# Gelus of the first block held as copies and made in one row, with one conversion buffer and a lower fill goal

## The chip, the cores and the metric

One core of one Trainium2 chip. The metric is the device time of the whole kernel in microseconds (us), lower is better.

## The reference, cut to what matters

```python
# attention: q, k, v of (batch 8, heads 8, seq 576, head_dim 64)
scores = scale * q @ k.T
scores = np.where(scores >= max(scores) - tau, scores, -1e9)
attn = exp(scores - max(scores)); attn = attn / (attn.sum() + 1e-9)
x = (attn @ v), transposed to (4608 tokens, 512)
# MLP: d_model 512, d_ff 2048, exact gelu
return gelu(x @ w_in) @ w_out
```

## The kernel before

Attention runs in **slots**: a slot is one chunk of 128 queries (or the 64 left over) of one pair of heads. The first batch, slots 0 to 19, covers four pairs; its probabilities are turned (transposed, and divided by their sums on the way) by TensorE with a diagonal of the reciprocal sums, from slot 20 on by VectorE and transfers. VectorE also converts the weights, which come as 64-bit floats, within the first batch. Whatever TensorE time is left is filled with matmuls of the MLP: a block is 256 tokens, and `GOAL` says how many blocks should be done by which slot. A block's layer one (`hT`) needs gelus, and each gelu needs another table of ScalarE than the exps of the softmax. `table()` puts the exp's table back by a dummy exp. In the lines of the profile, `sc` are scores, `tr` turned probabilities in PSUM (the memory into which the matmuls of this kernel write), `pT` their copy outside it, `diag` the diagonal, `xT` the attention's result in PSUM and `x` its copy, `g` a gelu's result, `o_ps` layer two. An engine *stands* while it idles for another's result or buffer; the *row* is the eight gelus that the change makes one after another.

```python
    late = []
    lag = [1]
    dirty = [False]
    def gelus(left):
        while len(late) > left:
            g, j, hT = late.pop(0)
            t = gp.tile([P, 2, TOK], FP32, tag="g", name="g")
            nc.scalar.activation(t, hT, AF.Gelu)
            g[j - 1], g[j] = t[:, 0, :], t[:, 1, :]
            dirty[0] = True
    def table():
        if dirty[0]:
            nc.scalar.activation(warm[:, 1:2], warm[:, 0:1], AF.Exp)
            dirty[0] = False

    def block_steps(n):
        g = {}
        mlp["layer"] = 1
        for j in range(N_DF):
            if j % 2 == 0:
                hT = None
            for c in range(N_DM):
                yield NS_IN, (j * P // PIECE + 1) * N_DM
                if hT is None:
                    hT = ps.tile([P, 2, TOK], FP32, tag="mm", name="hT")
                nc.tensor.matmul(hT[:, j % 2, :], lhsT=w_in_sb[c][:, j * P:(j + 1) * P], rhs=x_blk[n][:, c, :],
                                 start=(c == 0), stop=(c == N_DM - 1))
            if j % 2:
                late.append((g, j, hT))
                gelus(lag[0])
        for m in range(TOK // P):
            for j in range(N_DF):
                mlp["layer"] = 2
                yield NS_OUT, len(pieces) - N_DF + j + 1
                if j not in g:
                    gelus(0)
                if j == 0:
                    o = ps.tile([P, 512], FP32, tag="mm", name="o_ps")
                nc.tensor.matmul(o[:, 0:d_model], lhsT=g[j][:, m * P:(m + 1) * P], rhs=w_out_sb[j],
                                 start=(j == 0), stop=(j == N_DF - 1))
            o_sb = op.tile([P, d_model], FP32, tag="o_sb", name="o_sb")
            nc.scalar.copy(o_sb, o[:, 0:d_model])
            row = n * TOK + m * P
            nc.sync.dma_start(out[row:row + P, :], o_sb)
    # ... (cut)
    GOAL = [(-1, 0.0), (START - 1, 0.0), (BATCH - 1, 0.55)]      # BATCH = 20, START = 10
```

In each slot (cut; the whole order matters, since every engine takes its instructions in this order):

```python
        early = p < EARLY
        last = slots[n - 1] if 0 < n <= len(slots) else None
        if p < NP:
            scores(p, i)
            softmax_head(p, i)
        elif n == len(slots):
            ext = weights_in()
        if not early or n % 2 == 0:
            gelus(0)
            table()
        # ... weigh_v of what is due; if early: fill(owed, tokens); table()
        # ... turn_p_early of the slot before; softmax_tail
        convert(3000 if n < 2 * HP else 3650 if n < BATCH - 1 else 1e9)
        if early:
            diagonal(p, i)
```

The turn of the first batch and the conversion of a piece of weights (cut):

```python
    def turn_p_early(p, i):
        s = st[p]
        if i == 0 or (p < HP and i == 2):
            s["pT"] = [one.tile([P, KR, S], FP32, tag=f"pT{e}", name=f"pT{e}") for e in range(2)]
        w, diag = s.pop(("p", i)), s.pop(("diag", i))
        n = 1 if i == NC else 2
        def turn(to, cols, e):
            nc.tensor.matmul(to, lhsT=w[:, cols], rhs=diag[:, e, :], start=True, stop=True)
        for e in range(n):
            tr = ps.tile([P, NC, P], FP32, tag="mm", name="tr")
            for c in range(NC):
                at = e * (S + TAIL) + c * P
                turn(tr[:, c, :], slice(at, at + P), e)
            if i < NC:
                nc.scalar.copy(s["pT"][e][:, 0:NC, i * P:(i + 1) * P], tr)
        if i == NC:
            for e in range(2):
                nc.vector.tensor_copy(s["pT"][e][:, 0:NC, MAIN:S], tr[:, :, e * TAIL:(e + 1) * TAIL])
        tails = s["pT"][0][:, NC, :]
        tr = ps.tile([P, NC, P], FP32, tag="mm", name="tr")
        if i < NC:
            for e in range(2):
                at = MAIN + e * TAIL
                turn(tr[e * TAIL:(e + 1) * TAIL, 0, :], slice(at, at + TAIL), e)
            nc.scalar.copy(tails[:, i * P:(i + 1) * P], tr[:, 0, :])
            return
        turn(tr[0:TAIL, 0, :], slice(MAIN, S), 0)
        for e in range(2):
            rows = slice(e * TAIL, (e + 1) * TAIL)
            nc.vector.tensor_copy(tails[rows, MAIN:S], tr[0:TAIL, 0, rows])
```

```python
        vec = nc.vector
        ahead = None
        while raws or ahead:
            piece = None
            if raws:
                dst, raw, shifted = raws.pop(0)
                hi = raw.rearrange("p (f w) -> p f w", w=2)[:, :, 1]
                top = shifted.rearrange("p (f w) -> p f w", w=2)[:, :, 0]
                expo, power = (gp.tile([P, PIECE], U32, tag="g", name=s) for s in ("expo", "power"))
                vec.tensor_scalar(expo, hi, 0x7FF00000, None, op0=ALU.bitwise_and)
                nc.scalar.activation(power, expo, AF.Relu, bias=rebias, scale=8.0)
                piece = dst, hi, top, power
                yield 340
            if ahead:
                dst, hi, top, power = ahead
                mant = gp.tile([P, PIECE], U32, tag="g", name="mant")
                vec.tensor_scalar(mant, top, 0x0FFFFFFF, 0x10000000, op0=ALU.bitwise_and, op1=ALU.bitwise_or)
                yield 340
                vec.scalar_tensor_tensor(power, hi, 0x80000000, power, op0=ALU.bitwise_and, op1=ALU.bitwise_or)
                yield 720
                vec.scalar_tensor_tensor(dst, mant, 2.0 ** -28, power.bitcast(FP32), op0=ALU.mult, op1=ALU.mult)
                load_piece()
                converted[0] += 1
                yield 700
            ahead = piece
```

`ps` has four buffers of tag "mm" in PSUM, shared by `hT`, `o_ps`, `xT` and the turns' `tr`; `gp` has ten buffers of tag "g", shared by the gelus' results and the scratch of the conversions.

## Time and profile before

| | before |
|---|---|
| median of 3 runs | 1420.45 us (1420.29 to 1422.51) |
| span of the profiled run | 1421.8 us |
| TensorE busy / idle | 1382.1 / 39.7 us |
| ScalarE table loads in the trace | 144 of 1.283 us |

The profile's page gives busy time by engine and by fortieths of the span; tables of stretches give the same for any stretch, with the granted clock of TensorE; the list of waits says which instruction ended an engine's idle time (engine, tile and line that waited, what it waited for, then us in total, times, longest); the timeline has each instruction with its start, length and, in brackets, the idle time before it and what ended that. The lines that matter stand in the prediction. One more of before, the timeline of TensorE at the worst wait (start, length, what, count):

```profile
149.31 1.05 PE L302 MATMUL tr<-diag,p 128*128 128x128 f32 x8
152.65 2.70 PE L302 MATMUL tr<-diag,p 128*128 128x128 f32 x12 [2.28 <-ACT g L509]
155.28 2.29 PE L356 MATMUL sc<-pd_tail,q_tail 128*128 128x288 f32 x4
157.36 4.50 PE L543 MATMUL o_ps<-w_out,g 128*128 128x512 f32 x8
```

TensorE stands 2.28 us in the middle of a turn, until the gelu on ScalarE gives a PSUM buffer back; after it, four score matmuls take 2.29 us where the same four take 1.24 at 129.09, since the clock has fallen.

### The profile page before, as it was taken

Reading aid. Unit: us, or ns where it says so; the run is one execution under the profiler, and the core shown is the slowest. Engines: PE = TensorE matmul, PEld = TensorE weight load, DVE = VectorE, ACT = ScalarE, POOL = GpSimd, SP = SyncE. Lnnn points to the kernel's source line nnn. Section 1 sums busy time; section 2 is a strip of 40 time slices with the busy share of each in tenths; the row PEclk is TensorE's granted clock in tenths of the full one; section 3 lists DMA queues with packets and bytes.
Section 4 is the critical chain, followed back from the end, with each engine's and each line's share of the span. In section 5 each row is a group of like instructions: output and inputs, shape, how many; then the busy total and the mean of one; then the engine's idle time right before and its main releaser. Section 6 shows DMA issues by size and latency. Waiting matters only on the chain.

```text
span 1421.8 us, 19662 instructions
## 1 busy us (share of the span) xinstructions
PE 1382.1 (97%) x6544; PEld 958.8 (67%) x6544; DVE 892.6 (63%) x1788; ACT 640.9 (45%) x1040; POOL 388.0 (27%) x812
## 2 busy tenths in 40 slices
PE   6898999999999999999999999999999999999999
PEld 4666547566466574665756647566588888888887
DVE  5887777777777777777777777777764142241330
ACT  5758525436356273462645727547141140230320
POOL 4443244434433433434434434430000000000000
PEclk9999999999999999999999999999999999999999
DMA  9977167776666676666766666674500000001000
GB/s 265 295 264 243 38 145 150 148 156 129 134 136 148 146 156 129 146 135 149 162 148 146 158 146 150 141 160 101 106 3 8 23 1 26 19 1 48 12 8 23
DMA packets 219347, 167.05 MB, mean 117 GB/s; under 512 B 122480, under 2 KB 203952, under 8 KB 219248
## 3 DMA queue, kind: packets, MB, share of 16 engines
q1 hardware_dynamic: 193040, 108.65, 36.2%
q0 software_dynamic: 23808, 56.57, 13.1%
q8 instruction: 53, 0.87, 0.3%
q10 hardware_dynamic: 2400, 0.59, 0.2%
q14 instruction: 46, 0.38, 0.1%
HBM read 71.68 MB, written 11.47 MB: 58 GB/s over the span
## 4 chain that ended last, share of the span: by engine, by line
PE 87%; DVE 5%; ACT 5%; DMA 2%; issue 1%; SPq 0%; POOL 0%; DVEq 0%; ACTq 0%; POOLq 0%
PE bank L663 27%; PE o_ps L543 18%; PE hT L530 18%; PE sc L356 12%; PE xT L473 10%; ACT p L371 1%; DVE p L387 1%; PE tr L302 1%; DVE power L187 1%; DMA q<-in_q_dram 1%; DVE nmx L368 1%; ACT L509 1%; ACT diag L401 1%; DMA turned_p<-in_moe_w_in_dram 1%; ACT power L179 0%
## 5 line engine op out<-in xcount | busy, mean ns | idle before, releaser
L371 ACT ACTIVATE p<-sc,nmx 128x576 f32<-128x576 f32 x288 | 202.4, 739 | 383.9 <-DVE nmx L368 383.8
L368 DVE TENSOR_REDUCE nmx<-sc 128x1 f32<-128x576 f32 x288 | 205.0, 749 | 158.8 <-PE sc L356 158.7
L530 PE MATMUL hT<-x,w_in 128*128 128x256 f32 x1280 | 296.2, 384 | 0.0
L543 PE MATMUL o_ps<-w_out,g 128*128 128x512 f32 x640 | 295.1, 604 | 0.0
L530 PEld LDWEIGHTS hT<-x,w_in 128*128 128x128 f32 x1280 | 238.4, 190 | 56.4 <-issue 24.7
L387 DVE SCALAR_TENSOR_TENSOR p<-sc,thr,p 128x576 f32<-128x576 f32 x288 | 225.4, 816 | 65.2 <-ACT p L371 64.1
L369 POOL TENSOR_SCALAR thr<-nmx,tau_eff 128x1 f32<-128x1 f32 x288 | 84.3, 293 | 547.7 <-DVE nmx L368 547.6
L543 PEld LDWEIGHTS o_ps<-w_out,g 128*128 128x128 f32 x640 | 117.1, 190 | 140.0 <-issue 138.2
L356 PE MATMUL sc<-kT,qT 64*128 64x288 f32 x960 | 165.9, 435 | 2.8 <-DVE p L387 2.5
L473 PE MATMUL xT<-pT,v 128*64 128x256 f32 (+1 forms) x1280 | 163.7, 409 | 2.7 <-ACT g L509 2.7
L434 DVE STREAM_TRANSPOSE turned_p<-p 128x1152 f32<-128x1152 f32 x112 | 154.1, 1376 | 3.0
L356 PEld LDWEIGHTS sc<-kT,qT 64*128 64x128 f32 x960 | 93.7, 188 | 84.2 <-issue 71.8
L473 PEld LDWEIGHTS xT<-pT,v 128*64 128x64 f32 x1280 | 89.8, 137 | 74.1 <-issue 12.7
L234 POOL DMA_DIRECT2D v<-in_v_dram x208 | 110.5, 534 | 10.7 <-issue 9.8
L663 PE MATMUL bank<-x,w_in 128*128 128x256 f32 x384 | 93.3, 379 | 0.0
L663 PE MATMUL bank<-w_out,unit 128*128 128x256 f32 x416 | 92.4, 379 | 0.0
L516 ACT ACT_TABLE_LOAD x71 | 91.1, 1283 | 1.3
L509 ACT ACT_TABLE_LOAD x71 | 91.1, 1283 | 1.2
L663 PEld LDWEIGHTS bank<-w_out,unit 128*128 128x128 f32 x416 | 79.0, 190 | 10.7
L663 PEld LDWEIGHTS bank<-x,w_in 128*128 128x128 f32 x384 | 73.0, 190 | 10.3 <-issue 0.5
L225 POOL DMA_DIRECT2D q<-in_q_dram x104 | 70.7, 685 | 16.0 <-issue 15.1
L302 PE MATMUL tr<-diag,p 128*128 128x128 f32 (+1 forms) x360 | 51.4, 311 | 19.6 <-ACT diag L401 11.4
(148 smaller groups left out, 1326.8 us busy)
## 6 DMA issues: line engine op xcount, KB each, us to landing
pT<-turned_p SPq DMA_DIRECT2D x448, 160.0 KB, 3.6
pT<-pd_tail SPq DMA_DIRECT2D x112, 80.0 KB, 2.9
q<-in_q_dram POOLq DMA_DIRECT2D x104, 72.0 KB, 4.1
k<-in_k_dram POOLq DMA_DIRECT2D x104, 72.0 KB, 2.6
inv<-turned SPq DMA_DIRECT2D x56, 128.0 KB, 3.9
v<-in_v_dram POOLq DMA_DIRECT2D x156, 40.0 KB, 3.3
out_dram<-o_sb SPq DMA_DIRECT2D x20, 256.0 KB, 4.4
raw<-in_moe_w_in_dram POOLq DMA_DIRECT2D x8, 512.0 KB, 5.2
```

The lines of the kernel that those rows point to most:

```text
L234: eng.dma_start(t[r:P:4, e, 0:n, :], rows[:, r * KR:r * KR + n, :])
L356: nc.tensor.matmul(sc[e][:, h, 0:HALF], lhsT=lhsT, rhs=s["kT"][rows, at:at + HALF], start=True, stop=True)
L368: nc.vector.tensor_reduce(nmx[:, e:e + 1], sc, axis=AXIS.XY, op=ALU.max, negate=True)
L371: nc.scalar.activation(w[:, e * S:(e + 1) * S].rearrange("p (h s) -> p h s", h=2), sc, AF.Exp, bias=nmx[:, e:e + 1], scale=1.0)
L387: nc.vector.scalar_tensor_tensor(row, sc[e][:, :, 0:HALF], thr[:, e:e + 1], row, op0=ALU.is_ge, op1=ALU.mult, accum_out=den[e])
L434: nc.vector.transpose(turned_p[:, :, i // 2, 0:NB, i % 2 * Q:(i % 2 + 1) * Q], w.rearrange("p (e b i) -> p e b i", e=2, i=Q))
L473: nc.tensor.matmul(to, lhsT=s["v"][:, e, c, :], rhs=rhs, start=(c == 0), stop=(c == KR - 1))
L509: nc.scalar.activation(t, hT, AF.Gelu)
L516: nc.scalar.activation(warm[:, 1:2], warm[:, 0:1], AF.Exp)
L530: nc.tensor.matmul(hT[:, j % 2, :], lhsT=w_in_sb[c][:, j * P:(j + 1) * P], rhs=x_blk[n][:, c, :], start=(c == 0), stop=(c == N_DM - 1))
L543: nc.tensor.matmul(o[:, 0:d_model], lhsT=g[j][:, m * P:(m + 1) * P], rhs=w_out_sb[j], start=(j == 0), stop=(j == N_DF - 1))
L663: nc.tensor.matmul(to, lhsT=l, rhs=r, start=start and k == 0, stop=k == len(pairs) - 1, skip_group_check=not start)
```

## The change

In the first batch, the results of layer one are only copied out of PSUM (a copy needs no table); the eight gelus are made in one row, in place, at slot 20. For the buffers this takes, a conversion uses one scratch buffer instead of three. Besides: the small tail copies go from VectorE to ScalarE, the scaling of q has its own step one slot sooner, finished blocks are put away in memory one per slot, the last tile of layer one is emptied at the start of every slot and not of every second one, and the goal of the first batch is 0.50 of a block instead of 0.55, which is just its layer one.

```diff
--- before.py
+++ after.py
@@ -174,14 +174,13 @@
                 dst, raw, shifted = raws.pop(0)
                 hi = raw.rearrange("p (f w) -> p f w", w=2)[:, :, 1]
                 top = shifted.rearrange("p (f w) -> p f w", w=2)[:, :, 0]
-                expo, power = (gp.tile([P, PIECE], U32, tag="g", name=s) for s in ("expo", "power"))
-                vec.tensor_scalar(expo, hi, 0x7FF00000, None, op0=ALU.bitwise_and)
-                nc.scalar.activation(power, expo, AF.Relu, bias=rebias, scale=8.0)
-                piece = dst, hi, top, power
+                power = gp.tile([P, PIECE], U32, tag="g", name="power")
+                vec.tensor_scalar(power, hi, 0x7FF00000, None, op0=ALU.bitwise_and)
+                nc.scalar.activation(power, power, AF.Relu, bias=rebias, scale=8.0)
+                piece = dst, hi, top, dst.bitcast(U32), power
                 yield 340
             if ahead:
-                dst, hi, top, power = ahead
-                mant = gp.tile([P, PIECE], U32, tag="g", name="mant")
+                dst, hi, top, mant, power = ahead
                 vec.tensor_scalar(mant, top, 0x0FFFFFFF, 0x10000000, op0=ALU.bitwise_and, op1=ALU.bitwise_or)
                 yield 340
                 vec.scalar_tensor_tensor(power, hi, 0x80000000, power, op0=ALU.bitwise_and, op1=ALU.bitwise_or)
@@ -310,7 +309,7 @@
                 nc.scalar.copy(s["pT"][e][:, 0:NC, i * P:(i + 1) * P], tr)
         if i == NC:
             for e in range(2):
-                nc.vector.tensor_copy(s["pT"][e][:, 0:NC, MAIN:S], tr[:, :, e * TAIL:(e + 1) * TAIL])
+                nc.scalar.copy(s["pT"][e][:, 0:NC, MAIN:S], tr[:, :, e * TAIL:(e + 1) * TAIL])
         tails = s["pT"][0][:, NC, :]
         tr = ps.tile([P, NC, P], FP32, tag="mm", name="tr")
         if i < NC:
@@ -322,7 +321,11 @@
         turn(tr[0:TAIL, 0, :], slice(MAIN, S), 0)
         for e in range(2):
             rows = slice(e * TAIL, (e + 1) * TAIL)
-            nc.vector.tensor_copy(tails[rows, MAIN:S], tr[0:TAIL, 0, rows])
+            nc.scalar.copy(tails[rows, MAIN:S], tr[0:TAIL, 0, rows])
+
+    def scale_q(p):
+        t = st[p]["q"]
+        nc.scalar.activation(t, t, AF.Copy, bias=0.0, scale=q_scale)
 
     def turn_qk(p):
 
@@ -335,7 +338,6 @@
         qt = s["q_tail"] = q_tail[p % 4]
         qs, ks = s.pop("q"), s.pop("k")
         nc.vector.transpose(kT.rearrange("p (b i) -> p b i", i=Q), ks)
-        nc.scalar.activation(qs, qs, AF.Copy, bias=0.0, scale=q_scale)
         nc.vector.transpose(
             qT.rearrange("p (c a i) -> p c a i", c=NC, i=Q),
             qs[:, 0:MAIN // Q, :].rearrange("p (a c) j -> p c a j", c=NC))
@@ -501,14 +503,31 @@
     late = []
     lag = [1]
     dirty = [False]
+    held = []
+    hold = [True]
+
     def gelus(left):
+
 
         while len(late) > left:
             g, j, hT = late.pop(0)
             t = gp.tile([P, 2, TOK], FP32, tag="g", name="g")
-            nc.scalar.activation(t, hT, AF.Gelu)
-            g[j - 1], g[j] = t[:, 0, :], t[:, 1, :]
-            dirty[0] = True
+            if hold[0]:
+                nc.scalar.copy(t, hT)
+                held.append((g, j, t))
+            else:
+                gelu(g, j, t, hT)
+
+    def gelu(g, j, t, src):
+        nc.scalar.activation(t, src, AF.Gelu)
+        g[j - 1], g[j] = t[:, 0, :], t[:, 1, :]
+        dirty[0] = True
+
+    def gelus_held():
+        hold[0] = False
+        while held:
+            g, j, t = held.pop(0)
+            gelu(g, j, t, t)
 
     def table():
 
@@ -538,6 +557,7 @@
                 yield NS_OUT, len(pieces) - N_DF + j + 1
                 if j not in g:
                     gelus(0)
+                    gelus_held()
                 if j == 0:
                     o = ps.tile([P, 512], FP32, tag="mm", name="o_ps")
                 nc.tensor.matmul(o[:, 0:d_model], lhsT=g[j][:, m * P:(m + 1) * P], rhs=w_out_sb[j],
@@ -784,7 +804,7 @@
     WEIGH = 2
     START = 2 * HP + 2
 
-    GOAL = [(-1, 0.0), (START - 1, 0.0), (BATCH - 1, 0.55)]
+    GOAL = [(-1, 0.0), (START - 1, 0.0), (BATCH - 1, 0.5)]
     GOAL += [(BATCH * (m + 2) + WEIGH, x) for m, x in enumerate([1.96, 3.3, 4.64, 5.98, 7.32, 8.66, PLAIN])]
 
     def goal(n):
@@ -799,6 +819,7 @@
     tokens = 0
     owed = 0.0
     due = []
+    leaving = []
     loads = iter(())
     for n in range(len(slots) + WEIGH + 1):
         p, i = slots[n] if n < len(slots) else divmod(n, SLOTS)
@@ -809,9 +830,10 @@
             softmax_head(p, i)
         elif n == len(slots):
             ext = weights_in()
-        if not early or n % 2 == 0:
-            gelus(0)
-            table()
+        gelus(0)
+        if n == BATCH:
+            gelus_held()
+        table()
         made = []
         for args in due:
             weigh_v(*args)
@@ -859,6 +881,8 @@
             loads = load_steps(p + 2)
         if p >= HP:
             next(loads, None)
+        if p >= HP and i == 1 and p + 1 < NP or p == HP - 1 and i == 2:
+            scale_q(p + 1)
         if p >= HP - 1 and i == 2 and p + 1 < NP:
             turn_qk(p + 1)
         convert(3000 if n < 2 * HP else 3650 if n < BATCH - 1 else 1e9)
@@ -879,9 +903,9 @@
             tokens = S
         elif p > EARLY and i == WEIGH and p % HP == 0:
             tokens = p // HP * S
-            for n in AWAY:
-                if n in x_blk and (n + 1) * TOK <= tokens:
-                    put_away(n)
+            leaving += [n for n in AWAY if n in x_blk and (n + 1) * TOK <= tokens]
+        elif leaving and i < 2:
+            put_away(leaving.pop(0))
     fill(1e12, B * S)
     strassen(*ext)
```

## The prediction

> **What bounds the kernel now.** I read the page first (busy shares and the 40 slices), then the waits of TensorE, then tables of stretches, then the timelines of TensorE, ScalarE and VectorE between 70 and 185 us. The page says that TensorE is nearly always busy, except at the start:
>
> ```profile
> PE 1382.1 (97%) x6544; PEld 958.8 (67%) x6544; DVE 892.6 (63%) x1788; ACT 640.9 (45%) x1040; POOL 388.0 (27%) x812
> ...
> PE   6898999999999999999999999999999999999999
> ...
> PEclk9999999999999999999999999999999999999999
> ```
>
> Idle TensorE time is 1421.8 - 1382.1 = 39.7 us in all, so no change of order can win more than that plus what the clock loses. By the tables of stretches 14.0 us of the idle lie before 36 us and about 5.3 us between 36 and 71 us (loads and first diagonals; the change doesn't touch them), and about 5.4 us in the last stage. What the change touches is the second half of the first batch, slots 8 to 19. In the trace that runs from about 66 us to 164 us; slot 20's scores begin at 163.95. The one long stretch in which everything changes is from the scores of slot 10 (77.76) to those of slot 20, and then on to the scores of slot 22 (179.45):
>
> ```profile
> 77.76:163.95 86.19, 77.97 (x433) 58.42 (x431) 65.73 (x149) 62.22 (x107) 29.18 (x59) 0.94 0.62 204
> 163.95:179.45 15.50, 14.82 (x67) 7.13 (x65) 10.95 (x21) 7.56 (x13) 4.66 (x14) 1.00 0.14 33
> ```
>
> Columns: length; busy us (instructions) of TensorE, its weight loads, VectorE, ScalarE, GpSimd; granted clock; DMA share; GB/s. In the first row TensorE is idle 86.19 - 77.97 = 8.2 us and runs at 0.94 of the clock, which costs 86.19 x 0.06 = 5.2 us more: 13.4 us of loss. What ended the idle time there (TensorE's waits in that stretch):
>
> ```profile
> PE tr L302 <- ACT g L509: 5.0, 4, 2.3
> PE tr L302 <- ACT pT L310: 2.4, 3, 0.8
> PE tr L302 <- ACT x L488: 0.7, 1, 0.7
> ```
>
> All 8.1 us wait for ScalarE: the turns of the probabilities find no free PSUM buffer until ScalarE has emptied one. ScalarE's timeline shows why it is late:
>
> ```profile
> 97.36 1.28 ACT L509 ACT_TABLE_LOAD   x1
> 98.65 0.60 ACT L509 ACTIVATE g<-hT 128x512 f32<-128x512 f32 x1
> 99.27 1.28 ACT L516 ACT_TABLE_LOAD   x1
> 100.56 0.20 ACT L516 ACTIVATE warm<-warm 128x1 f32<-128x1 f32 x1
> ...
> 150.71 1.28 ACT L509 ACT_TABLE_LOAD   x1
> 152.00 0.60 ACT L509 ACTIVATE g<-hT 128x512 f32<-128x512 f32 x1
> ```
>
> A single gelu holds ScalarE from 97.36 to 100.67, 3.3 us. This comes eight times, from 97 to 171 us. After 164 us TensorE waits little: 2.7 us for gelus (twice 1.35, at 327 and 421 us), 2.5 us for VectorE ahead of scores, 2.1 us in the last stage.
>
> **What the Trainium skill says.** (1) "ScalarE: Activation LUTs", section What ACT_TABLE_LOAD costs: about 1283 ns a load, plus a drain of about 1380 ns. The trace agrees with 1.28 us; it shows no drain of that size, since the gelu starts 0.01 us after the load's end. I use 1.28. (2) Same page, section Table sets: the hidden batching unit: batch calls by set; cheap functions such as copy are in every set. So copies cost no load. (3) "TensorE: Matmul & The Clock Gate", section Part 1: an idle window of about 3.4 us halves the clock. The trace shows this with shorter idles: TensorE stood 2.28 us before 152.65 and the clock was 0.54 and 0.60 in the two next stretches of 4 us. (4) Same page, section Architectural detail: ScalarE and VectorE are strict FIFO; it matters for slot 20 below.
>
> **The change part by part** (counts from the order of instructions of the two built programs).
>
> Gelus: all eight (gelu plus two loads plus the dummy exp: 3.3 us) become eight copies of the same 128x512 tile, 0.59 us as the copies of that shape take. ScalarE gets back 8 x 2.7 = 22 us in slots 12 to 20. The row in slot 20 costs 1.28 + 8 x 0.55 + 1.28 + 0.2 = 7.2 us. Loads in the program fall from 144 to 136 only, since later gelus stand more often alone; there ScalarE has room.
>
> Conversions: same instructions, one scratch buffer where there were three. That takes away VectorE's waits of the mantissa step for a free buffer: 6.2 us in three waits between 74 and 166 us. It is also needed, as eight g buffers of ten stay held until slot 20.
>
> Tail copies: four small copies per pair go from VectorE (1.1 us a pair) to ScalarE, which has the time now. Scaling q one slot sooner removes a 0.3 us VectorE wait. Putting blocks away one per slot moves transfers at 400 us and later that TensorE doesn't wait for today: 0.
>
> Goal 0.50 for 0.55: slots 10 to 19 hold 6 or 7 pairs of hT matmuls instead of 7 or 8, and slot 19 has the last 6 pairs of hT where 4 pairs of o_ps stood. Nothing is removed; it comes later.
>
> TensorE's floor from the scores of slot 10 to those of slot 20: 77.97 - 5.2 (clock) - 8 x 0.45 (the o_ps records that leave) = 69.2 us. VectorE's floor there, from its timeline: 5.8 us for a one-chunk slot, 6.5 us for a two-chunk slot without tail copies, each with its own wait for the exp: 4 x 5.8 + 6 x 6.5 + 2 for the turn of q and k = 64 us. But it starts 3 us behind (its first reduction of slot 10 comes at 81.70, while the scores were ready at 79.0), so the two run close, and I leave 3 us of waits and lost clock out of today's 13.4. Slot 20's scores then start at 77.8 + 69.2 + 3 = 150.0, where they start at 163.95 today.
>
> Slot 20, counted from its scores at T: exps end at T + 3.45 (as today, 167.4 - 163.95), the last copy at T + 4.05, load T + 5.35, first gelu T + 5.95. TensorE has scores and ten turns to do until T + 3.4, then stands for **2.5 us**; from then on a gelu (0.55 us) feeds two o_ps matmuls, four records of 0.45 us, so TensorE doesn't catch up with the row. Ten o_ps records end at T + 10.4, scores of slot 21 at T + 11.6. The tail copies of pT stand behind the gelus and the second load, ready at T + 12.4, so xT stands **0.8 us**. Then xT 2.84 and ten o_ps 4.5: the scores of slot 22 come at T + 19.8. I add 1.5 us for the clock, as an idle of 2.3 us cost 3.4 us of clock at 152 to 160 us (0.46 x 4 + 0.40 x 4), but not each does. So slot 22's scores start at 150.0 + 21.3 = 171.3 instead of 179.45.
>
> By then 6 records of o_ps fewer are done (20 against 26), 6 x 0.43 = 2.6 us, which TensorE pays later. Gain: 179.45 - 171.3 - 2.6 = **5.5 us**. Later stages: one of the two waits of 1.35 us may go as gelus come one by one: 0.5. Sum 1420.45 - 6 = **1414.5 us**.
>
> **The rivals.** *The new bubble eats the gain.* The row of gelus puts 3.3 us of standing at one place, with FIFO order behind it and a cold clock (to 3 us), and if pT is later than I have it, slot 22 too. For it: today's worst wait is of this same form. Against: eight waits go for one. Then the gain is 1 to 3 us, 1418 to 1420. *VectorE becomes the bound of slots 8 to 19.* Its floor is within 5 us of TensorE's, and the reciprocals and diagonals that release the turns come after 3.65 us of conversions. For it: before 97 us the chain of waits runs over VectorE's steps already. Then slot 20's scores come near 153: 1417. *Everything falls into place*: no clock loss in slot 20 and under 1 us of waits before: 1410 to 1411. *The deferred work finds idle time later*: TensorE idles 1.5 us from 178 to 249 us, and 3.0 us from 320 to 500; at best 1 us more.
>
> **Range and chances.** The floor is 1420.45 - 13.4 - 2.7 = 1404 with nothing lost in slot 20; two per cent is 28 us, over twice all that the region loses. A loss would need new waits of over 13 us. So 1409.5 to 1419 for 8 in 10; within 2% is 0.98, 0.01 on either side.
>
> **What would show it.** Right: no gelu and no table load from 75 us until one row of eight near 152 us; TensorE's waits for g in the turns gone, the clock near 1.0 from 98 to 150 us; scores of slot 20 near 150; a stand of 2 to 3 us ahead of the first o_ps; VectorE's mantissa step without waits. Wrong: turns waiting for the diagonals instead (VectorE bound), stands over 4 us at slot 20 with a clock near 0.5 for 7 us, new waits for pT or for x after 180 us, or slots 0 to 9 changing at all.

## The result

| | before | changed |
|---|---|---|
| median | 1420.41 us (1420.29 to 1422.51, 4 runs) | 1414.90 us (1413.93 to 1416.21, 4 runs) |
| span of the profiled run | 1421.8 us | 1412.1 us |
| TensorE idle in the profiled run | 39.7 us | 35.1 us |

The ratio is 0.9958 (95% interval 0.9941 to 0.9976): faster by 0.4%, and within 2%. A ratio is the mean time of one kernel's fast runs over that of the other's of the same rounds, so it isn't quite the ratio of the medians. In five later rounds on another chip (run e12) the kernel before took 1422.2 to 1425.3 us and the changed one 1414.86: 0.9936. So the gain is 0.4 to 0.6%, 6 to 9 us by the ratios. The two profiled runs differ by 9.7 us in their spans: the one of before (1423.59 us in device time) was the slowest of its kernel there and the one of the changed kernel (1413.93) its fastest.

The changed kernel's page, busy time by engine:

```profile
PE 1377.0 (98%) x6544; PEld 956.6 (68%) x6544; DVE 886.8 (63%) x1772; ACT 636.3 (45%) x1052; POOL 389.0 (28%) x812
```

The same two stretches, from the scores of slot 10 (78.78) over those of slot 20 (150.84) to those of slot 22 (169.77); columns as in the prediction:

```profile
78.78:150.84 72.06, 69.79 (x424) 53.89 (x423) 62.16 (x137) 45.26 (x98) 30.33 (x59) 1.00 0.76 245
150.84:169.77 18.93, 15.75 (x68) 7.56 (x66) 9.57 (x17) 13.20 (x26) 4.66 (x14) 1.00 0.12 27
```

The first took 86.19 us and takes 72.06; TensorE idles 2.3 us in it instead of 8.2, and the clock is full (1.00, where before had 0.94). How much of that clock is the held gelus' doing isn't shown: the run e2 below, whose waits for ScalarE are nearly those of before (8.8 us), kept a full clock in the same stretch and took 4 us less for it than before:

```profile
77.38:159.61 82.23, 73.35 (x433) 55.29 (x431) 66.61 (x151) 61.82 (x107) 29.38 (x59) 1.00 0.66 215
```

The second stretch took 15.50 and takes 18.93: that is the price. TensorE's waits in the first stretch are now:

```profile
PE tr L301 <- ACT g L516: 1.9, 1, 1.9
PE tr L301 <- ACT diag L403: 0.2, 1, 0.2
```

Of the eight stands for g, pT and x one of 1.9 us is left, in slot 18. Its copy of hT comes late because ScalarE's steps ahead of it idled 1.61, 1.33 and 0.34 us for VectorE (at 136.93, 138.99 and 140.05), so VectorE is behind this stand too. ScalarE at the place that the prediction showed, and at the row:

```profile
97.07 0.58 ACT L516 COPY g<-hT 128x512 f32<-128x512 f32 x1
97.53 0.50 ACT L490 COPY x<-xT 128x256 f32<-128x256 f32 x2
...
154.80 1.28 ACT L522 ACT_TABLE_LOAD   x1
156.09 4.26 ACT L522 ACTIVATE g<-g 128x512 f32<-128x512 f32 x8
160.37 1.28 ACT L535 ACT_TABLE_LOAD   x1
```

The copy holds ScalarE under 0.6 us instead of 3.3; all eight gelus take 4.26 us in a row. TensorE around the row:

```profile
150.84 1.24 PE L358 MATMUL sc<-kT,qT 64*128 64x288 f32 x8
152.26 1.52 PE L301 MATMUL tr<-diag,p 128*128 128x128 f32 x10 [0.18 <-ACT diag L403]
156.78 4.56 PE L563 MATMUL o_ps<-w_out,g 128*128 128x512 f32 x10 [3.00 <-ACT g L522]
161.27 1.24 PE L358 MATMUL sc<-kT,qT 64*128 64x288 f32 x8
162.44 2.92 PE L475 MATMUL xT<-pT,v 128*64 128x320 f32 x20
```

It stands 3.00 us for the first gelu. From slot 22's scores to the first matmuls of the last stage both kernels take 849.34 us (179.45 to 1028.79, and 169.77 to 1019.11), though the changed one has six o_ps records (2.6 us) more to do there. So the trace's account is: first ten slots +1.0, the next ten -14.1, slots 20 and 21 +3.4, all the rest 0: -9.7 us.

### The profile page after: what moved, and what is told of

It reads as the page before. It is cut to its first block, busy times and chain, and to the rows that moved or that the text cites. A ratio compares the mean times of both kernels' runs of the same rounds, so it can differ in the third digit from the quotient of the medians.

```text
span 1412.1 us, 19647 instructions
## 1 busy us (share of the span) xinstructions
PE 1377.0 (98%) x6544; PEld 956.6 (68%) x6544; DVE 886.8 (63%) x1772; ACT 636.3 (45%) x1052; POOL 389.0 (28%) x812
## 4 chain that ended last, share of the span: by engine, by line
PE 91%; DVE 4%; ACT 3%; DMA 2%; issue 1%; SPq 0%; POOL 0%; DVEq 0%; ACTq 0%; POOLq 0%
PE bank L683 27%; PE hT L549 20%; PE o_ps L563 19%; PE sc L358 12%; PE xT L475 10%; PE tr L301 2%; DVE p L389 1%; ACT p L373 1%; DMA q<-in_q_dram 1%; DVE power L186 1%; DMA turned_p<-in_moe_w_in_dram 1%; DVE nmx L370 0%; DVE w_in L188 0%; ACT diag L403 0%; DVE power L178 0%
## 5 line engine op out<-in xcount | busy, mean ns | idle before, releaser
L224 POOL DMA_DIRECT2D k<-in_k_dram x104 | 69.6, 675 | 0.7 <-DMA inv<-turned 0.3
```

The source lines that it names most:

```text
L224: eng.dma_start(t[e * D + f:e * D + f + Q], rows[:, :, f:f + Q])
```

## The experiments

Each run took five rounds against the kernel before (five runs of each kernel, but six of e6 and four of e10 and e11), in three calls: e1 to e4 (before: median 1422.42), e5 to e9 (1421.32), e10 to e12 (1424.68). Numbers of different calls are compared by their ratios; the changed kernel itself had 0.9958 in one call and 0.9936 in another, so across calls a difference under some 3 us can't be told.

| run | median us | ratio to before (95%) |
|---|---|---|
| e1 gelus not held | 1421.24 | 0.9993 (0.9981 to 1.0006) |
| e2 conversion buffers alone | 1421.20 | 0.9987 (0.9974 to 1.0000) |
| e3 goal 0.55 | 1415.77 | 0.9956 (0.9942 to 0.9970) |
| e4 table loads put back | 1426.51 | 1.0032 (1.0019 to 1.0044) |
| e5 tail copies on VectorE | 1416.29 | 0.9957 (0.9945 to 0.9969) |
| e6 putting away and scaling as before | 1415.84 | 0.9961 (0.9947 to 0.9974) |
| e8 conversions shifted later | 1413.18 | 0.9934 (0.9922 to 0.9947) |
| e9 goal 0.453 | 1416.18 | 0.9958 (0.9946 to 0.9970) |
| e12 changed kernel again | 1414.86 | 0.9936 (0.9922 to 0.9949) |
| e10 shift, last gelu from PSUM | 1412.17 | 0.9917 (0.9903 to 0.9930) |
| e11 larger shift | 1412.71 | 0.9921 (0.9908 to 0.9935) |

**The theory:** table loads in ScalarE's queue kept PSUM buffers from the turns. The rivals: VectorE's freed conversion buffers, the lower goal, the tail copies, or the small moves carry the gain.

### e1: everything but the held gelus

```diff
-    hold = [True]
+    hold = [False]
```

> The changed kernel with its gelus of the first block made at once again, as before the change (two table loads around each); conversions in one buffer, tail copies on ScalarE, goal 0.50 and the rest stay changed. Theory (the table loads in ScalarE's queue made the turns wait for PSUM buffers): most of the gain goes, 1418.5 to 1421 us, and TensorE again waits some 5 us or more for g and pT ahead of the turns between 78 and 165 us. Rivals (the gain comes from the freed conversion buffers, the tail copies or the smaller goal): it stays at 1414 to 1416.5 us.

Measured 1421.24 us, ratio 0.9993: no gain to be told from zero. TensorE's waits from 78 to 173 us:

```profile
PE tr L301 <- ACT g L522: 4.1, 1, 4.1
PE xT L475 <- ACT pT L312: 1.8, 2, 1.4
PE tr L301 <- ACT x L490: 1.3, 2, 0.7
PE tr L301 <- ACT pT L309: 0.8, 1, 0.8
```

The time is 0.2 us above the expected range. The stands for ScalarE are back, 8 us in all; 1.8 us of them wait for the tail copies' results and not for a buffer. All other parts of the change together, the emptying in every slot among them, win nothing without the held gelus.

### e2: the conversion buffers alone

The kernel before with the first hunk of the diff and nothing else.

> The kernel before with one part of the change: conversions in one scratch buffer, in place. Theory: VectorE's 6 us of waits of the mantissa step go, but TensorE's waits for ScalarE stay, so within 1.5 us of the kernel before: 1419 to 1421 us. Rival (VectorE's waits were the cause): 1414 to 1416.5 us.

Measured 1421.20 us, ratio 0.9987, whose interval ends at 1.0000: 0.2 us above the expected range; a gain of up to 3.7 us (0.9974) isn't excluded, the whole gain of the change is (e3 of the same rounds has 0.9942 to 0.9970). VectorE's wait of the mantissa step is gone from its list (it had 6.2 us; the next step's wait for ScalarE grew from 1.7 to 3.0), but TensorE's waits for ScalarE's buffers, here from 75 to 186 us, are nearly those of before:

```profile
PE tr L301 <- ACT g L508: 5.0, 4, 2.3
PE tr L301 <- ACT pT L309: 2.3, 3, 0.8
PE tr L301 <- ACT x L487: 1.5, 2, 0.7
```

Freeing an engine that isn't waited for moved its idle time and, as far as five runs can tell, little more.

### e3: the goal back at 0.55

```diff
-    GOAL = [(-1, 0.0), (START - 1, 0.0), (BATCH - 1, 0.5)]
+    GOAL = [(-1, 0.0), (START - 1, 0.0), (BATCH - 1, 0.55)]
```

> The changed kernel with the goal of the first batch back at 0.55, so that layer two starts in slot 19 and the row of gelus moves there. Theory: the goal only moves 2.8 us of TensorE work; the row's stand comes one slot sooner and the turns of slot 19 stand behind it: 1415 to 1418 us, still faster than before by over 2 us. Rival (the smaller goal is where the gain comes from): 1419 us or more.

Measured 1415.77 us, ratio 0.9956. The row now falls in slot 19 and the stand before the first o_ps is longer (5.64 us instead of 3.00, in the timeline), yet the time is that of e5 and e6, within the spread. The lower goal isn't where the gain comes from (the rival expected 1419 us or more).

### e4: two table loads put back at each copy

```diff
                 held.append((g, j, t))
+                nc.scalar.activation(warm[:, 1:2], warm[:, 0:1], AF.Gelu)
+                dirty[0] = True
```

> The changed kernel with a dummy gelu and a dummy exp after each held copy, which puts two table loads (together some 3 us of ScalarE) back at each of the eight places, with the copies, the row and all else as changed; the result stays right. Theory: the stands of 78 to 150 us come back while the stand at the row stays: 1421 to 1426 us, slower than the kernel before. Rivals: 1414 to 1417 us, since their parts are untouched.

Measured 1426.51 us, ratio 1.0032: slower than before, 0.5 us above the expected range, some 11 us slower than e3 in the same rounds. Copies, row, buffers and goal are untouched, only the loads (and two one-column dummies) are back. TensorE's waits from 78 to 173 us:

```profile
PE tr L301 <- ACT x L490: 3.4, 2, 2.2
PE o_ps L565 <- ACT g L524: 3.1, 1, 3.1
PE tr L301 <- ACT g L516: 2.6, 1, 2.6
PE xT L475 <- ACT pT L312: 2.1, 2, 1.5
PE tr L301 <- ACT pT L309: 1.2, 1, 1.2
```

There are fourteen loads more than in the changed kernel (the eighth pair serves the row itself), 14 x 1.28 = 18 us of ScalarE, and they cost about 11 us of time, held against e3; the rest fell into ScalarE's idle time. With e1, this shows that the table loads are the cause. That they act through PSUM buffers is read from the waits: a turn that waits for a copy of g, x or pT waits for the buffer which that copy empties. No run changed the number of buffers. 2.1 us here (xT for pT) wait for a result instead.

### e5: the tail copies back on VectorE

```diff
-                nc.scalar.copy(s["pT"][e][:, 0:NC, MAIN:S], tr[:, :, e * TAIL:(e + 1) * TAIL])
+                nc.vector.tensor_copy(s["pT"][e][:, 0:NC, MAIN:S], tr[:, :, e * TAIL:(e + 1) * TAIL])
-            nc.scalar.copy(tails[rows, MAIN:S], tr[0:TAIL, 0, rows])
+            nc.vector.tensor_copy(tails[rows, MAIN:S], tr[0:TAIL, 0, rows])
```

> The changed kernel with the sixteen tail copies back on VectorE (they are 1.1 us a pair there). Theory (ScalarE's table loads were the cause, and VectorE has a little room in slots 8 to 19): at most 1.5 us slower than the changed kernel: 1414 to 1417 us. Rival (VectorE's relief by these copies carries the gain): 1418 us or more.

Measured 1416.29 us, ratio 0.9957, the same as e3 and e6 within the spread. The tail copies don't carry the gain. This run's profile shows something else: TensorE stands for the row as long as in the changed kernel, but what follows takes 7.15 us instead of 4.56:

```profile
154.71 7.15 PE L563 MATMUL o_ps<-w_out,g 128*128 128x512 f32 x10 [3.00 <-ACT g L522]
```

Stretches of 4 us of the same run (length, busy us of the five engines, clock, DMA share, GB/s) show why:

```profile
154.00:158.00 4.00, 3.29 (x4) 1.50 (x5) 1.65 (x5) 3.99 (x9) 0.00 (x0) 0.50 0.00 0
158.00:162.00 4.00, 4.00 (x9) 1.45 (x9) 0.00 (x0) 1.78 (x3) 0.00 (x0) 0.76 0.00 0
```

The clock fell to half after the stand. Behind the same 3.00 us it stayed full in the profiles of the changed kernel and of e6, and fell in those of e5 and e8. Ten o_ps records took 4.56 us at full clock, 7.15 in e5 and 7.60 in e8. So a part of the spread of single runs, 2.6 to 3.0 us, lies here; that it explains each run's time isn't shown, as only one run of each has a profile.

### e6: putting away and scaling as before

The last hunk but one and the scaling of the diff undone: blocks put away in one slot, q scaled within the slot of its transposes.

> The changed kernel with two parts undone: blocks put away all in one slot again, and q scaled in the slot of its transposes again. Theory: TensorE waited for neither, so the time of the changed kernel within 1 us: 1414 to 1416 us, and no TensorE wait for transfers between 400 and 1000 us. Rival (the later stages gained by these): 1417 us or more.

Measured 1415.84 us, ratio 0.9961. No gain of these can be told; TensorE waits for no transfer of x in either.

### e9: the goal at 0.453, to fill the stand

```diff
-    GOAL = [(-1, 0.0), (START - 1, 0.0), (BATCH - 1, 0.5)]
+    GOAL = [(-1, 0.0), (START - 1, 0.0), (BATCH - 1, 0.453)]
```

> The changed kernel with the goal of the first batch at 0.453, so that six hT matmuls are left for slot 20 and TensorE has 2.7 us of work while the row of gelus starts. Theory (the stand at the row is real loss that other work can fill): the stand of 3.0 us before the first o_ps shrinks below 0.6 us and the end comes 1 to 2.5 us sooner: 1412.5 to 1414 us. Rival (slots 10 to 19 are bound by VectorE's steps, so taking work out of them only makes TensorE stand there): no gain, 1415 to 1417 us.

Measured 1416.18 us, ratio 0.9958: a miss. The stand is filled, as TensorE's waits from 78 to 170 us show, but others came:

```profile
PE tr L301 <- ACT diag L403: 1.5, 3, 0.7
PE xT L475 <- ACT pT L312: 1.1, 1, 1.1
PE tr L301 <- ACT x L490: 0.8, 1, 0.8
PE sc L358 <- DVE p L389: 0.3, 1, 0.3
PE tr L301 <- ACT g L516: 0.2, 1, 0.2
```

3.9 us of waits stand where the changed kernel has about 5.3 (1.9 for g, 3.0 at the row, 0.4 for diagonals). Taking work out of slots 10 to 19 let TensorE run up to VectorE's diagonals, and the tail copies behind the row held up xT. That left too little to be told from the spread.

### e8: conversions shifted out of the first eight slots

```diff
-        convert(3000 if n < 2 * HP else 3650 if n < BATCH - 1 else 1e9)
+        convert(2600 if n < 2 * HP else 3950 if n < BATCH - 1 else 1e9)
```

> The changed kernel with less conversion in slots 0 to 7 (2600 ns instead of 3000 a slot) and more in slots 8 to 18 (3950 for 3650). It asks what bounds the first ten slots, where TensorE still stands 7 us for diagonals. If VectorE does: slot 10 starts 2 to 3 us sooner, and as TensorE bounds slots 10 to 19 now, the end comes 1 to 2.5 us sooner, 1412.5 to 1414 us. If loads do, or if slots 10 to 19 turn VectorE-bound: 1415 us or more.

Measured 1413.18 us, ratio 0.9934, 2.7 us of median under e6 of the same rounds. In its trace the scores of slot 10 start at 75.17 us (78.78 in the changed kernel, 76.57 in e5, 78.84 in e6), and TensorE's waits for diagonals from 36 to 75 us fall from 7.0 to 4.5 us. The start is the better sign: in the unshifted runs of the changed kernel and its variants, e1, e3 to e6, e9 and e12, it lies between 76.57 and 78.86 us, and it is sooner in all three shifted ones (75.17 here, 75.98 in e10, 72.93 in e11), while the waits for diagonals vary (5.5 us in the unchanged e12, 5.0 in e10 and e11). So conversions on VectorE held up the first ten slots, and slots 10 to 19 have room for some of them.

### e12, e10, e11: a version that beats both

e12 is the changed kernel, unchanged.

> The changed kernel once more, unchanged, to be compared with the next two on the same chip and to see whether the clock falls after the stand of slot 20 in this profile: 1414 to 1416.5 us; the stand before the first o_ps again 3.0 us.

e10 has the shift of e8 and makes the last tile's gelu straight from PSUM at the end of the row:

```diff
-        gelus(0)
         if n == BATCH:
             gelus_held()
+        gelus(0)
```

> The changed kernel with conversions shifted from slots 0 to 7 into slots 8 to 18 (2600 and 3950 ns a slot) and the row of gelus ahead of the last tile, whose gelu is then made straight from PSUM, so that the first o_ps needn't wait for that copy. The stand before the first o_ps should be 2.4 us instead of 3.0; 1412 to 1413.5 us, some 2 us under the changed kernel of these rounds (2 from the shift, as measured alone, up to 0.6 from the stand).

e11 is e10 with 2250 and 4200.

> The same with a larger shift (2250 and 4200 ns a slot). If slots 10 to 19 still have room on VectorE: another 1 us, 1411 to 1412.5 us. If VectorE bounds them by then: TensorE waits for diagonals or scores of over 3 us between 75 and 150 us, and 1412.5 to 1414.5 us.

Measured: e12 1414.86, e10 1412.17, e11 1412.71 us. The stand at the row was 3.25 us in e12 (with a full clock after it) and 2.53 in e10:

```profile
154.47 6.16 PE L563 MATMUL o_ps<-w_out,g 128*128 128x512 f32 x10 [2.53 <-ACT g L522]
```

e10 gains 2.7 us over the changed kernel of the same rounds, though its clock fell after the stand in this profile. What the direct gelu adds to the shift can't be told: e8 and e10 ran in different calls. The larger shift gains no more: in e11 TensorE waits 2.4 us for diagonals and 0.9 for scores from 75 to 186 us (1.5 us together in e10), so VectorE holds TensorE up there by then. In this profile the clock also fell between 84 and 100 us (0.73 and 0.84 in two stretches of 8 us), so the loss isn't VectorE's alone. Both are faster than the kernel before and e10 than the changed one; e10 has the lowest median, from which e11 can't be told.

## Why the prediction was right

It put 1414.5 us with 1409.5 to 1419; the median was 1414.90. The mechanism held; that the number is off by only 0.4 us is in part luck, as the sum after the list shows. The signs that it named for being right all came: no table load from 75 us until the one at 154.80, a clock of 1.00, slot 20's scores at 150.84, a stand of 3.00 us ahead of the first o_ps, no wait of the mantissa step. Slot 10 starts 1.0 us later, which it called a sign of being wrong; that lies within the runs' spread (76.57 to 78.86 us). By its steps:

- **What holds TensorE up.** Shown: the waits for g, pT and x fell from 8.1 to 1.9 us, e1 brings them back with all other parts in place, and e4 brings the loss back by the loads alone.
- **Slots 10 to 19.** A floor of 69.2 us and 3 us of waits: 72.2; measured 72.06, of which 69.79 busy and 2.3 idle. The remaining stand is listed under another name than it expected, g in slot 18 and not diagonals, though VectorE is behind it. Its base was a dear one: the 86.19 us of before hold some 4 us of clock that e2 didn't lose with nearly the same waits.
- **Slot 20.** First o_ps at T + 5.95: measured 156.78 - 150.84 = 5.94. TensorE was done with the turns at T + 2.94 and not 3.4, so it stood 3.00 us and not 2.5. Scores of slot 21 done at T + 11.6: measured 11.60 (162.44). The stand of 0.8 us for xT isn't there: the eight gelus took 4.26 us and not 4.4, the tail copies began at T + 10.9 and ended at T + 11.9 and not 12.4, and xT could start before the last of them. So slot 22 came at T + 18.93 and not 19.8.
- **The clock after the row.** 1.5 us as an average of falling and not falling; shown in kind, as the profiles have 0 (changed kernel, e6), 2.6 (7.15 - 4.56, e5) and 3.0 us (7.60 - 4.56, e8) after the same stand. How often it falls isn't known.
- **Later stages.** It gave 0.5 us for one of the waits of 1.35 us. Wrong term: both are there in the changed kernel too (2.7 us, in two). Instead the waits of scores for VectorE fell, from 2.5 to 1.5 us.
- **Conversions.** The waits of the mantissa step went, as expected, but e2 leaves them at most 3.7 us alone, and its means 1.9 us. The wait of VectorE for the scaled q, which was to lose 0.3 us, grew to 2.0 us, because the tail copies now stand ahead of the scaling in ScalarE's queue; in e5, with these copies on VectorE, it is gone.
- **Rivals.** The new bubble takes 3.0 us and sometimes the clock, as feared, but one stand replaced seven. VectorE isn't the bound at goal 0.50; e9 and e11 show that it is close.

The gain of the profiled pair, 9.7 us, is larger than the timed 5.5; held against the traces alone the predicted 6 us would be 3.7 too small. The clock, which didn't fall after the row in this profile, and the missing stand of xT are 2.4 of that (21.3 against 18.93). Slot 20 came 0.84 late, and the 2.6 us of deferred work don't show in the later stages: 1.0 us less idle time pays for a part there, and the rest I can't place. So errors of 2.4 and 2.6 us stand against others of 0.8 and 0.5, and the forecast took a gain worked out from the slowest run of before off a median that is 3.1 us faster than that run; in the later rounds the same change was worth 9 us.

## What to carry to other kernels

Ask what an instruction keeps occupied while it waits for a table, not what it costs: here eight gelus of 0.6 us held ScalarE 3.3 us each, and with it the PSUM buffers that it was to empty, and the engine behind those buffers stood. If results aren't needed soon, get them out of the scarce memory with an operation that needs no table, and make the costly function later in one row. Then look for what the row itself holds up: its first result, not its length, sets the new stand.

## What the Trainium skill lacked or had wrong

- "ScalarE: Activation LUTs", What ACT_TABLE_LOAD costs: a drain of about 1380 ns beside each load. In these runs the gelu starts 0.01 us after a load of 1.28 us (97.36 + 1.28 and 98.65 before; 154.80 + 1.28 and 156.09 changed), so a switch there and back cost 2.6 us and not 5.3.
- "TensorE: Matmul & The Clock Gate", Part 1: an idle window of about 3.4 us makes the clock fall. Here it fell after stands of 1.38 us (e1: the xT matmuls after it took 4.67 us, where 2.91 is usual), 2.28 (before) and 2.53 us (e10), well below that, but not after 2.29 (e2), 2.51 (e11) and 3.25 us (e12), and after a stand of 3.00 us in two profiles and not in two others. So the length of one stand doesn't decide it; the page tells of short idles too, but gives no length for them. The page has the window running freely, which fits that it depends on the run.
- No page has a measured cost of one such stand for float32 matmuls of 512 columns: ten o_ps records took 4.56 us at full clock, and 6.16 (e10), 7.15 (e5) and 7.60 us (e8) after the clock fell.
